# A first batch rearranged: kv products of one head pair by single heads, a sine scaling moved to GpSimd, one weight cast on ScalarE, the last weight slice cast in whole pieces

## Chip, core and metric

Each run used one core of a Trainium2 chip. The metric is the device time of one execution in microseconds (us). The jobs ran on several chips (5, 2, 12 and 3; that of the first job is not on record), so a ratio compares a kernel with the runs of before in its own job. PE is the tensor engine, PEld its weight loads, DVE the vector engine, ACT the scalar engine, POOL GpSimd, SP the engine whose queue issues the loads.

## The reference, cut to what matters

```python
# attention (8 batches, 8 heads, 576 positions, head size 64)
k_p = concat(relu(k) * cos, relu(k) * sin)        # same for q
kv  = einsum('bhsf,bhsd->bhfd', k_p, v);  z = sum(k_p, over s)
out = (q_p @ kv) / (q_p @ z + 1e-6)               # -> x, 4608 tokens x 512
# feed-forward
h = x @ w_in                                      # 512 -> 2048
g = h * sigmoid(beta * h)
return g @ w_out                                  # 2048 -> 512
```

## The kernel before

Tokens go through the feed-forward part in nine chunks of 512. For a chunk PE has 32 slots: 16 column groups of w_in (4 matmuls each), then 16 parts of w_out work. Before chunk 0 there is a head: attention of batch 0, while all weights are still being loaded (as float32, to be cast to bf16 by other engines). The casts of the four w_in slices (column groups 0 to 3, 4 to 7, ...) run on GpSimd and the DVE, just ahead of PE:

```python
def cast_win(i, gj, eng="dve", f0=0, f1=512, jps=slice(0, 2)):   # one of four pieces (g, jj) of slice i, 64 partitions
    ...
def cast_halves(i):
    for f in (0, 256):            # first half of the columns (two column groups), then the second
        for gj in GJ:
            cast_win(i, gj, "dve", f, f + 256)
```

In the head (cut):

```python
v_scale(0, 1, 0, 0, 6, eng="pool")        # sine part of v, head pair 0: 6 of 9 tiles on GpSimd
take("act", 1)
v_scale(0, 1, 0, 6, NQ, eng="act")        # the other 3 on ACT
v_scale(0, 0, 0)                          # cosine part, DVE
k_relu(0, 0, 2, "act", 0, 5);  k_relu(0, 0, 2, "dve", 5, NQ)
take("dve", 0)
kv_mm(0, 0, 6)                            # kv product of pair 0
...
k_relu(0, 2, 3, "act");  k_relu(0, 3, 4, "act", 5, NQ)     # head 2; rest of head 3
...
got = x_rden(2, 0, 0, 7, (0,)); got2 = x_rden(4, 0, 7, 8, (0,))   # denominators, DVE
k_relu(0, 3, 4, "dve", 0, 5)              # head 3, first 5 tiles
warm_pe(2, bank=1)
kv_mm(0, 1, 6)                            # kv product of pair 1: heads 2 and 3 together
```

`warm_pe(n)` puts n idle matmuls on PE, `GJ` lists the four pieces (g, jj) of a slice, `take` copies transposed q out of PSUM, `x_rden` makes the denominators and `x_mul` multiplies by them.

The weights pass through four staging buffers, so a w_out load waits until a w_in slice has been cast:

```python
cast_halves(2); cast_halves(3)
load_w("out", 0); load_w("out", 1)
load_raw(1, "v"); load_raw(1, "k"); load_w("out", 2); load_raw(1, "q"); load_w("out", 3)
```

Of the kernel before, what the change touches and what calls it, by code (L numbers as in the profile page):

```python
# [17 lines left out]
NQ = 9  # L18
# [4 lines left out]
def kernel(  # L23
# [46 lines left out]
    def raw_tile(b, name):  # L70
        if (name, b) not in raws:
            raws[name, b] = raw_pool.tile([P, 4, NQ, D], FP32, name=f"raw_{name}", tag=f"raw_{name}")
        return raws[name, b]
# [14 lines left out]
    def load_w(kind, i, step=4):  # L88
        if (kind, i) not in stages:
            stages[kind, i] = stage.tile([P, 4, 512], FP32, name="w_stage", tag="w_stage")  # L90
        st = stages[kind, i]
        if kind == "out":
            nc.sync.dma_start(out=st, in_=w_out_v[:, 4 * i : 4 * i + 4, :])
            return
        for a in range(0, 4, step):
            nc.sync.dma_start(out=st[:, a : a + step], in_=w_in_v[:, a : a + step, i * 512 : (i + 1) * 512])

    def cast_win(i, gj, eng="dve", f0=0, f1=512, jps=slice(0, 2)):

        g, jj = gj  # L100
        o = win[i].rearrange("q (jp g) f -> q jp g f", g=2)[jj * HP : (jj + 1) * HP, jps, g, f0:f1]
        a = stages["in", i].rearrange("q (jp jj) f -> q jp jj f", jj=2)[g * HP : (g + 1) * HP, jps, jj, f0:f1]
        if eng == "act":
            nc.scalar.copy(o, a)
        elif eng == "pool":
            nc.gpsimd.tensor_copy(o, a)
        else:
            nc.vector.tensor_copy(o, a)  # L108
# [11 lines left out]
    GJ = [(0, 0), (0, 1), (1, 0), (1, 1)]  # L120
# [65 lines left out]
    def relu(dst, src, eng):  # L186
        if eng == "act":
            nc.scalar.activation(dst, src, AF.Relu)  # L188
        else:
            nc.vector.tensor_scalar(dst, src, scalar1=0.0, scalar2=None, op0=ALU.max)  # L190

    def q_relu(b, jp, eng="dve"):
        relu(qb[:, jp].rearrange("q n (j d) -> q j n d", j=2), raw_tile(b, "q")[:, 2 * jp : 2 * jp + 2], eng)

    def k_relu(b, j0=0, j1=4, eng="dve", n0=0, n1=NQ):
        relu(rk.rearrange("q n j d -> q j n d")[:, j0:j1, n0:n1], raw_tile(b, "k")[:, j0:j1, n0:n1], eng)

    def v_scale(b, cs, jp=None, n0=0, n1=NQ, eng="dve"):
        t = (cos9, sin9)[cs]
        rv = raw_tile(b, "v")  # L200
        js = slice(0, 4) if jp is None else slice(2 * jp, 2 * jp + 2)
        if jp is not None and eng != "act":
            if eng == "dve":
                t = ps[:, 0, 16 * cs : 16 * cs + NQ]
            (nc.gpsimd if eng == "pool" else nc.vector).tensor_tensor(
                vb[:, n0:n1, js, cs, 0:D],
                rv.rearrange("q j n d -> q n j d")[:, n0:n1, js],
                t[:, n0:n1].unsqueeze(2).unsqueeze(3).to_broadcast([P, n1 - n0, 2, D]), op=ALU.mult)
            return
        for n in range(n0, n1):  # L210
            o, a = vb[:, n, js, cs, 0:D], rv[:, js, n, :]
            if eng == "act":
                nc.scalar.activation(o, a, AF.Copy, scale=t[:, n : n + 1])  # L213
            else:
                nc.vector.tensor_scalar(o, a, scalar1=t[:, n : n + 1], scalar2=None, op0=ALU.mult)  # L215
# [35 lines left out]
    def kv_out(jp, bank):  # L251
        return ps[:, bank : bank + 2, jp * 2 * E : (jp + 1) * 2 * E]

    def kv_mm(b, jp, bank, jjs=(0, 1)):
        t = kv_out(jp, bank)
        for n in range(NQ):
            for jj in jjs:
                for g in range(2):
                    hs = slice(g * HP, (g + 1) * HP)
                    nc.tensor.matmul(  # L260
                        t[jj * HP : (jj + 1) * HP, g], lhsT=rk[hs, n, 2 * jp + jj, :],
                        rhs=vb[hs, n, 2 * jp + jj].rearrange("q s e -> q (s e)"),
                        start=(n == 0), stop=(n == NQ - 1))

    def kv_take(jps, bank, eng="dve"):
        a0, a1 = jps[0], jps[-1] + 1
        o = kv[:, :, a0:a1].rearrange("q g s c e -> q g (s c e)")
        a = ps[:, bank : bank + 2, a0 * 2 * E : a1 * 2 * E]
        if eng == "act":
            nc.scalar.copy(o, a)  # L270
        else:
            nc.vector.tensor_copy(o, a)  # L272

    def num_mm(n, jp, bank, slot):

        for cs in range(2):
            for jj in range(2):
                rows = slice(jj * HP, (jj + 1) * HP)
                for g in range(2):
                    cols = slice(g * HP, (g + 1) * HP)  # L280
                    nc.tensor.matmul(  # L281
                        ps[cols, bank + jj, slot * E : (slot + 1) * E],
                        lhsT=(qt, qs)[cs][rows, jp, n, cols],
                        rhs=kv[rows, g, jp, cs, :],
                        start=(cs == 0), stop=(cs == 1))

    def x_rden(bank, slot, n0, n1, jps):

        w, m = len(jps), n1 - n0
        nv = ps[:, bank : bank + 2, slot * E : (slot + w * m) * E].rearrange("q j (i s e) -> q j i s e", s=w, e=E)  # L290
        den = small.tile([P, 2, m, w], FP32, name="den", tag=f"den{m}{w}")
        nc.vector.tensor_tensor(  # L292
            den, nv[:, :, :, :, D],
            eps9[:, n0:n1].unsqueeze(1).unsqueeze(3).to_broadcast([P, 2, m, w]), op=ALU.add)
        rden = small.tile([P, 2, m, w], FP32, name="rden", tag=f"rden{m}{w}")
        nc.vector.reciprocal(rden, den)
        return nv, rden, n0, jps

    def x_mul(got, n0, n1):
        nv, rden, first, jps = got  # L300
        a, z, w = n0 - first, n1 - first, len(jps)
        o = xs[:, n0:n1, jps[0] : jps[-1] + 1].rearrange("q n s (j d) -> q j n s d", j=2)
        nc.vector.tensor_tensor(  # L303
            o.rearrange("q j n s d -> q j (n s) d"),
            nv[:, :, a:z, :, 0:D].rearrange("q j n s d -> q j (n s) d"),
            rden[:, :, a:z].rearrange("q j n s -> q j (n s)").unsqueeze(3).to_broadcast([P, 2, (z - a) * w, D]),
            op=ALU.mult)

    def x_mul_act(got, n):
        nv, rden, first, jps = got  # L310
        for s_, jp in enumerate(jps):
            for jj in range(2):
                nc.scalar.activation(xs[:, n, jp, jj * D : (jj + 1) * D], nv[:, jj, n - first, s_, 0:D],
                                     AF.Copy, scale=rden[:, jj, n - first, s_ : s_ + 1])
# [99 lines left out]
    def warm_pe(count, w=512, bank=1):  # L414
        for i in range(count):
            nc.tensor.matmul(ps[:, bank, 0:w], lhsT=zeros[:, 0:P], rhs=zeros[:, 0:w], start=True, stop=True)  # L416
# [24 lines left out]
    warm_pe(7)  # L441
    take("act", 0)
    take("dve", 1)
    v_scale(0, 1, 0, 0, 6, eng="pool")
    take("act", 1)
    v_scale(0, 1, 0, 6, NQ, eng="act")
    v_scale(0, 0, 0)
    k_relu(0, 0, 2, "act", 0, 5)
    k_relu(0, 0, 2, "dve", 5, NQ)
# [4 lines left out]
    kv_take((0,), 6, eng="act")  # L454
    v_scale(0, 1, 1, 5, NQ, eng="act")
    k_relu(0, 2, 3, "act")
    k_relu(0, 3, 4, "act", 5, NQ)
    for i in range(1, 4):
        load_w("in", i)
    warm_pe(1)  # L460
    for n in range(7):
        num_mm(n, 0, 2, n)
    num_mm(7, 0, 4, 0)
    got = x_rden(2, 0, 0, 7, (0,))
    got2 = x_rden(4, 0, 7, 8, (0,))
    k_relu(0, 3, 4, "dve", 0, 5)
    warm_pe(2, bank=1)
    kv_mm(0, 1, 6)
    kv_take((1,), 6, eng="act")
    x_mul(got, 0, 7)  # L470
    x_mul_act(got2, 7)
    warm_pe(1, bank=1)
    for n in range(7):
        num_mm(n, 1, 0, n)
    num_mm(7, 1, 6, 0)
    for gj in GJ:
        cast_win(0, gj, "pool", jps=slice(0, 1))
    for gj in GJ:
        cast_win(0, gj, "pool", 0, 256, slice(1, 2))
    x_turn_pe(0, 0, 8, 2, jps=(0,))  # L480
# [1 line left out]
    x_mul(got, 0, 4)  # L482
    x_mul(got, 4, 7)
    x_mul(x_rden(6, 0, 7, 8, (1,)), 7, 8)
    warm_pe(3, bank=3)
    x_turn_pe(0, 0, 4, 4, ("act",), (1,))
    h_mm(0, 0, (0, 1))
    x_turn_pe(0, 4, 8, 5, ("act",), (1,))
# [5 lines left out]
    def cast_halves(i):  # L494
        for f in (0, 256):
            for gj in GJ:
                cast_win(i, gj, "dve", f, f + 256)
# [3 lines left out]
    def rest():  # L501

        x_mul(x_rden(2, 0, 8, NQ, (0, 1)), 8, NQ)
        cast_halves(2)
        cast_halves(3)
        load_w("out", 0)
        load_w("out", 1)
        load_raw(1, "v")
        load_raw(1, "k")
        load_w("out", 2)  # L510
        load_raw(1, "q")
        load_w("out", 3)
        cast_wout(0)
        cast_wout(1)
        v_scale(1, 0)
        k_relu(1)
        cast_wout(2)
        q_relu(1, 0)
# [111 lines left out]
```

## Time and profile before

| | before |
|---|---|
| time, three runs | 296.96 us (296.57 to 296.97) |
| span of the profiled run | 295.0 us |
| first w_in matmul, first w_out matmul | 18.06, 33.06 us |
| w_out 3 lands; PE's wait for its cast | 45.21 us; 0.33 us |
| second chunk's first matmul | 51.60 us |

All later stages are matmuls without a gap, so the row "second chunk" stands for the end: in the profiles of this study the rest takes 243.2 to 243.9 us.

### The profile page before, as it was taken

Reading aid. Unit: us, or ns where it says so; the run is one execution under the profiler, and the core shown is the slowest. Engines: PE = TensorE matmul, PEld = TensorE weight load, DVE = VectorE, ACT = ScalarE, POOL = GpSimd, SP = SyncE. Lnnn points to the kernel's source line nnn. Section 1 sums busy time; section 2 is a strip of 40 time slices with the busy share of each in tenths; the row PEclk is TensorE's granted clock in tenths of the full one; section 3 lists DMA queues with packets and bytes.
Section 4 is the critical chain, followed back from the end, with each engine's and each line's share of the span. In section 5 each row is a group of like instructions: output and inputs, shape, how many; then the busy total and the mean of one; then the engine's idle time right before and its main releaser. Section 6 shows DMA issues by size and latency. Waiting matters only on the chain.

```text
span 295.0 us, 7173 instructions
## 1 busy us (share of the span) xinstructions
PE 286.8 (97%) x3058; PEld 142.8 (48%) x3058; DVE 116.3 (39%) x296; ACT 140.1 (47%) x223; POOL 73.8 (25%) x88
## 2 busy tenths in 40 slices
PE   8799999999999999999999999999999999999994
PEld 7454455455445544454445544554455444444443
DVE  5989978662920293019500960077005000000000
ACT  5758826563247214731474137512760277137510
POOL 1350003252382026402550256015701210000000
PEclk9999999999999999999999999999999999999999
DMA  7999999597999089916992599139102810130033
GB/s 259 366 393 379 387 389 393 197 288 268 163 259 361 4 125 219 383 62 120 217 379 76 113 231 397 45 67 196 44 2 46 146 37 0 41 84 19 0 73 71
DMA packets 50256, 53.82 MB, mean 182 GB/s; under 512 B 30880, under 2 KB 31152, under 8 KB 50224
## 3 DMA queue, kind: packets, MB, share of 16 engines
q1 hardware_dynamic: 47504, 46.01, 51.6%
q0 software_dynamic: 2688, 7.34, 10.7%
q8 instruction: 24, 0.39, 0.6%
q14 instruction: 8, 0.07, 0.1%
q10 hardware_dynamic: 32, 0.01, 0.0%
HBM read 36.71 MB, written 9.44 MB: 156 GB/s over the span
## 4 chain that ended last, share of the span: by engine, by line
PE 85%; DVE 5%; DMA 5%; ACT 2%; issue 1%; DVEq 0%
PE ps L366 38%; PE ps L391 38%; DMA w_stage<-in_moe_w_out_dram 5%; DVE win L108 4%; PE ps L281 4%; PE ps L260 3%; PE ps L407 1%; PE ps L416 1%; ACT vb L213 1%; DVE qs L218 1%; DVE xs L303 0%; ACT g_t L373 0%; ACT rk L188 0%; PE ps L425 0%; PE ps L230 0%
## 5 line engine op out<-in xcount | busy, mean ns | idle before, releaser
L366 PE MATMUL ps<-xt,win 128*128 128x512 bf16 x576 | 128.1, 379 | 0.8 <-ACT g_t L373 0.5
L391 PE MATMUL ps<-wout,g_t 128*128 128x512 bf16 x560 | 124.5, 379 | 0.2 <-ACT wout L115 0.2
L373 ACT ACTIVATE g_t<-ps,beta 128x512 bf16<-128x512 f32 x144 | 98.4, 687 | 36.6 <-PE ps L366 36.6
L366 PEld LDWEIGHTS <-win 128*128 128x128 bf16 x576 | 55.3, 98 | 67.6 <-DVE win L108 1.4
L391 PEld LDWEIGHTS <-g_t 128*128 128x128 bf16 x560 | 53.9, 98 | 64.0 <-issue 0.4
L386 POOL DMA_DIRECT2D out_dram<-o_sb x56 | 36.5, 656 | 142.2 <-ACT o_sb L397 142.2
L397 ACT COPY o_sb<-ps 128x512 f32<-128x512 f32 x35 | 20.5, 586 | 98.2 <-PE ps L391 98.2
L218 POOL TENSOR_TENSOR qs<-qt,tanr 128x1152 bf16<-128x1152 bf16 x12 | 29.3, 2456 | 10.2 <-DMA qt<-qb 10.2
L272 DVE CAST kv<-ps 128x520 bf16<-128x520 f32 x6 | 4.2, 700 | 67.8 <-PE ps L260 67.8
L410 DVE COPY o_sb<-ps 128x256 f32<-128x256 f32 x1 | 0.4, 425 | 63.0 <-PE ps L407 63.0
L303 DVE TENSOR_TENSOR xs<-ps,rden 128x768 bf16<-128x768 f32 (+5 forms) x26 | 23.1, 890 | 0.8
L292 DVE TENSOR_TENSOR den<-ps,eps 128x12 f32<-128x12 f32 (+4 forms) x26 | 4.2, 161 | 33.5 <-PE ps L281 33.5
L215 DVE TENSOR_SCALAR vb<-raw_v,cos 128x256 bf16<-128x256 f32 x63 | 17.1, 347 | 0.0
L215 DVE TENSOR_SCALAR vb<-raw_v,sin 128x256 bf16<-128x256 f32 x54 | 14.7, 349 | 0.0
L281 PEld LDWEIGHTS <-qt 64*64 64x64 bf16 x576 | 10.6, 106 | 5.0 <-issue 4.3
L281 PE MATMUL ps<-kv,qt 64*64 64x65 bf16 x576 | 11.8, 195 | 0.4 <-ACT kv L270 0.2
L190 DVE TENSOR_SCALAR qb<-raw_q 128x1152 bf16<-128x1152 f32 x16 | 11.4, 752 | 1.3 <-DMA raw_q<-in_q_dram 1.3
L108 DVE CAST win<-w_stage 64x512 bf16<-64x512 f32 (+1 forms) x28 | 11.6, 414 | 0.6
L260 PE MATMUL ps<-vb,rk 64*64 64x130 bf16 x576 | 10.1, 218 | 1.6 <-ACT rk L188 1.6
L281 PE MATMUL ps<-kv,qs 64*64 64x65 bf16 x576 | 11.6, 193 | 0.0
L260 PEld LDWEIGHTS <-rk 64*64 64x64 bf16 x576 | 8.5, 106 | 5.7 <-issue 3.0
L281 PEld LDWEIGHTS <-qs 64*64 64x64 bf16 x576 | 10.4, 105 | 0.0
(56 smaller groups left out, 99.9 us busy)
## 6 DMA issues: line engine op xcount, KB each, us to landing
raw_v<-in_v_dram SPq DMA_DIRECT2D x7, 1152.0 KB, 10.2
raw_k<-in_k_dram SPq DMA_DIRECT2D x7, 1152.0 KB, 12.9
raw_q<-in_q_dram SPq DMA_DIRECT2D x7, 1152.0 KB, 7.4
out_dram<-o_sb POOLq DMA_DIRECT2D x56, 128.0 KB, 4.1
w_stage<-in_moe_w_out_dram SPq DMA_DIRECT2D x4, 1024.0 KB, 9.0
w_stage<-in_moe_w_in_dram SPq DMA_DIRECT2D x3, 1024.0 KB, 12.8
out_dram<-o_sb SPq DMA_DIRECT2D x14, 128.0 KB, 2.3
raw_q<-in_q_dram SPq DMA_DIRECT2D x2, 576.0 KB, 4.4
```

Of the source, the lines that this page charges most:

```text
L108: nc.vector.tensor_copy(o, a)
L190: nc.vector.tensor_scalar(dst, src, scalar1=0.0, scalar2=None, op0=ALU.max)
L215: nc.vector.tensor_scalar(o, a, scalar1=t[:, n : n + 1], scalar2=None, op0=ALU.mult)
L218: eng.tensor_tensor(dst.rearrange("q n (g p) -> q n g p", g=2), src.rearrange("q n (g p) -> q n g p", g=2), tanr[:, n0:n1].unsqueeze(2).to ...
L260: nc.tensor.matmul(t[jj * HP : (jj + 1) * HP, g], lhsT=rk[hs, n, 2 * jp + jj, :], rhs=vb[hs, n, 2 * jp + jj].rearrange("q s e -> q (s e)") ...
L281: nc.tensor.matmul(ps[cols, bank + jj, slot * E : (slot + 1) * E], lhsT=(qt, qs)[cs][rows, jp, n, cols], rhs=kv[rows, g, jp, cs, :], start ...
L303: nc.vector.tensor_tensor(o.rearrange("q j n s d -> q j (n s) d"), nv[:, :, a:z, :, 0:D].rearrange("q j n s d -> q j (n s) d"), rden[:, :, ...
L366: nc.tensor.matmul(ps[:, h_bank(c, jt)], lhsT=win[jt // 4][:, mi, (jt % 4) * P : (jt % 4 + 1) * P], rhs=xt[:, :, jp, g * HP : (g + 1) * HP ...
L373: nc.scalar.activation(g_t, ps[:, h_bank(c, jt)], AF.Silu, scale=beta[:, jt : jt + 1])
L386: eng.dma_start(out=out_v[bb, n][:, m0:m1], in_=o_sb[hf * HP : (hf + 1) * HP, m0:m1])
L391: nc.tensor.matmul(o_ps, lhsT=gs[c, jt][:, tt * P : (tt + 1) * P], rhs=wout[jt // 4][:, jt % 4, :], start=(jt == 0), stop=(jt == JT - 1))
L397: nc.scalar.copy(o_sb, o_ps)
```

## The change

Its intent: free ACT in the head (sine of pair 0 all on GpSimd), start head 2's kv product while head 3 is not ready, let GpSimd end its casts earlier, and save DVE time on the last slice (fewer, larger casts), which also issues the last w_out load earlier. The diff, with context cut:

```diff
-    v_scale(0, 1, 0, 0, 6, eng="pool")
+    v_scale(0, 1, 0, eng="pool")
     take("act", 1)
-    v_scale(0, 1, 0, 6, NQ, eng="act")
...
-    k_relu(0, 3, 4, "act", 5, NQ)
...
     num_mm(7, 0, 4, 0)
+    warm_pe(2, bank=1)
+    kv_mm(0, 1, 6, (0,))
+    k_relu(0, 3, 4, "act", 5, NQ)
     got = x_rden(2, 0, 0, 7, (0,))
     got2 = x_rden(4, 0, 7, 8, (0,))
     k_relu(0, 3, 4, "dve", 0, 5)
-    warm_pe(2, bank=1)
-    kv_mm(0, 1, 6)
+    kv_mm(0, 1, 6, (1,))
+    x_mul_act(got2, 7)
     kv_take((1,), 6, eng="act")
     x_mul(got, 0, 7)
-    x_mul_act(got2, 7)
-    warm_pe(1, bank=1)
...
-        cast_win(0, gj, "pool", jps=slice(0, 1))
+        cast_win(0, gj, "act" if gj == (1, 1) else "pool", jps=slice(0, 1))
...
-    warm_pe(3, bank=3)
+    warm_pe(2, bank=3)
...
         cast_halves(2)
-        cast_halves(3)
+        for gj in GJ:
+            cast_win(3, gj)
```

## The prediction

> **What bounds the kernel now.** I read the page first: busy shares, the chain, the costliest groups. The tensor engine (PE) is busy for 97% of 295.0 us and the chain is matmuls from 56 us to the end, so nothing in the steady part can change: the diff touches only the first batch's set-up and the casts of w_in, all before 32 us. A change there is worth what it moves of the time at which PE gets into that steady run. So I read next the chain in order of time, then the waits and the timeline of the first 56 us, then the landings of the transfers.
>
> The chain that ended last, in order of time, about 12 to 17 us and 31 to 46 us (columns: start us, us, what):
> ```profile
> 11.40 0.73 PE ps L260 x36
> ...
> 12.53 1.18 ACT vb L213 x4
> 13.71 0.57 ACT rk L188
> 14.29 0.04 issue
> 14.33 0.92 PE ps L260 x36
> 15.25 0.02 issue
> 15.27 0.39 ACT kv L270
> 15.66 0.04 issue
> 15.70 0.68 PE ps L281 x48
> ...
> 31.06 0.42 DVE win L108
> 31.48 0.03 issue
> 31.51 13.70 DMA w_stage<-in_moe_w_out_dram
> 45.21 0.02 issue
> 45.24 0.73 ACT wout L115
> 45.97 0.04 issue
> 46.01 1.02 PE ps L391 x4
> ```
> The reader is to see two things. The head is a hand-over between ACT and PE (sin part of v, relu of k, kv product, its copy). And the link at 31.51 us seems to say that the last w_out load starts when the last w_in cast ends, so that earlier casts would bring an earlier load. The next view says otherwise.
>
> Busy time by stretch (PE, PEld, DVE, ACT, POOL, clock, DMA share, GB/s):
> ```profile
> 18.00:24.00 6.00, 5.91 (x46) 2.80 (x45) 5.63 (x18) 4.27 (x8) 1.19 (x3) 1.00 1.05 387
> 24.00:32.00 8.00, 8.00 (x39) 3.25 (x38) 7.61 (x20) 6.29 (x11) 0.00 (x0) 1.00 1.03 374
> 32.00:46.00 14.00, 13.84 (x144) 7.15 (x143) 11.70 (x28) 7.78 (x17) 0.00 (x0) 1.00 1.05 392
> ```
> The DMA engines are full the whole way at 374 to 392 GB/s. In the trace the completions follow one another in the order of issue: w_in slice 3 at 24.44 us, w_out 0 at 27.29, w_out 1 at 29.98, v 33.10, k 36.11, w_out 2 at 38.82, q 41.84, w_out 3 at 45.21. Each comes 2.7 to 3.4 us after the one before, and each was issued long before its predecessor landed (w_out 3 at 31.51, 10 us before q landed). So 13.7 us is queueing: w_out 3 lands at about 45.2 us whenever it is issued. PE is ready for it at 45.68 us (last matmul start 45.465 plus 0.216 of streaming) and starts at 46.01: 0.33 us of waiting. A PE that is earlier at this point gains nothing; one that is later by up to 0.33 us loses nothing.
>
> Groups and waits of the first 56 us:
> ```profile
> L108 DVE CAST win<-w_stage 64x512 bf16<-64x512 f32 x24 | 10.1, 421 | 0.5
> L108 DVE CAST win<-w_stage 64x256 bf16<-64x256 f32 x4 | 1.5, 370 | 0.1
> L205 POOL TENSOR_TENSOR vb<-raw_v,sin 128x768 bf16<-128x768 f32 x1 | 1.5, 1473 | 6.9 <-ACT qt L235 6.9
> ```
> ```profile
> PEld L366 <- DVE win L108: 1.4, 4, 0.4
> ```
> From 26 to 31.5 us PE follows the DVE's casts, but barely: eight casts per slice, half a slice (two column groups) per 1.77 us, against 1.73 us of matmuls (8 by 0.216). The weight loads wait 4 times; the matmul starts in the trace show what reaches PE: 0.17 us at column group 8 (25.83 to 26.22 instead of 0.216) and 0.04 us at groups 10, 12 and 14. PE starts w_out work at 33.06 us.
>
> **What the Trainium skill says.** "SBUF — State Buffer", section "SBUF: two separate sides": DVE and GpSimd share one port pair under an exclusive lock. The trace agrees: a 64x256 cast takes 288 and 292 ns after GpSimd has finished, 472 and 430 ns beside its casts. "VectorE: DVE Perf Modes", the section on the TRN2 errata, measures a fixed part of about 150 cycles, so 512 elements at two per cycle would be (150+256)/0.96 = 423 ns; the row has 421. "TensorEngine Tiling (Array Packing)", "Key Properties": tiles run in parallel. The trace agrees: the kv matmuls start four at a time 3 ns apart, one such step per 56.5 ns, which is the 130 columns. "DMA: Bandwidth & Descriptors", "Queues, rings and completion order", says that descriptors are consumed in ring order on each engine; the landings above agree.
>
> **The change part by part.**
> 1. *Sin of pair 0 all on GpSimd.* ACT loses three 128x128 scalings, 0.99 us by the timeline. GpSimd grows from 768 to 1152 elements: 1473 ns for 768 and 1261 for 640 give 1.66 ns each, so 2.11 us from 9.06, ending near 11.17, or 11.3 if the lock with the DVE's relu (10.43 to 10.85) costs. ACT's relu of k can start when k lands (10.40) instead of 10.63 and ends at 11.15 instead of 11.35. The first kv product then starts at about 11.25, not 11.40: 0.15 us gained, and ACT's next work (bounded by v's landing at 12.14) is earlier by about as much. Head 2's relu ends near 14.13 instead of 14.28.
> 2. *kv of pair 1 by heads.* Before, head 2 was held back by head 3: its first two matmuls went at 14.33, the next at 14.53, after the DVE's relu of head 3 (14.01 + 0.47 = 14.48), and the last at 15.01. Now head 2 can go at 14.18. But one head uses two of four tiles, and a step still streams 130 columns: 9 steps are 0.08 + 8 x 0.0565 = 0.53 us per head, not per pair. Head 3 starts at about 14.66 and its last step at 15.14 us: about 0.13 us later than before. Splitting costs more streaming (0.5 us) than the head start hides (0.3 us). The two ACT scalings of xs move from after the kv copy to before it (0.53 us in ACT's idle time); the filler matmuls removed (0.22 us each) lay in waits. So I take the rest of the head, up to the start of the w_in matmuls, as 0.1 to 0.15 us late.
> 3. *One cast piece on ACT.* GpSimd loses one of four 64x512 pieces at 0.66 us and ends at 18.66 instead of 19.32. ACT takes it in a gap (15.7 to 17.0 us). GpSimd is then done before the DVE's four quarter casts begin: those take 4 x 0.31 = 1.24 us instead of 1.57 (18.55 to 20.12). The DVE's train gains 0.33 us, less the 0.14 of step 2: 0.19. The 0.17 us wait at column group 8 goes.
> 4. *Slice 3 in whole pieces.* Four casts of 64x1024: 421 ns plus 512 elements at the slope of the two rows without contention (421-290 over 256 elements, 0.51 ns) is 0.68, with issue 0.71; four are 2.84 us against eight at 0.443, 3.54. The DVE saves 0.70 us and is free at 30.6 rather than 31.5. But column group 12 needed only the first half, ready at 29.74 us; now it needs all four. The DVE starts the slice at 27.97 - 0.19 = 27.78, the pieces for the first row block are there at 29.2, the others at 30.62. PE is at group 12 at 29.29 + 0.14 = 29.43, does one matmul and waits until 30.66. Then 7 matmuls as before from 31.54 to 33.06 (1.52), plus 8 by 0.216 (1.73): PE starts w_out work at 33.91, not 33.06, 0.8 us late. This is the largest term.
>
> From 33.06 to 45.68 PE has no wait in the trace (only two switches of 0.1 us), so it arrives at w_out 3 at 46.5 us. The slack takes 0.33 of the 0.8. ACT's and the DVE's takes of q lie before their w_out 3 casts and are set by PE, so these casts slip too, to about the same time; the last of the DVE's three may cost another 0.1. Sum: 0.5 to 0.6 us later. The waits at 51.60 (0.39 in matmul starts) and 56.60 (0.66) are for work of ACT that PE itself released, so they move along and absorb nothing.
>
> **The rivals.** *A: hidden by the DMA, no change.* If the casts are fast or the head gains 0.4 us more than I find, PE is late by under 0.33 us, w_out 3 at 45.2 sets the start, and the time stays at 296.9. For it: the full DMA. Against: the 1.2 us between halves and whole pieces at group 12. *B: the earlier issue pays, faster by 0.5 to 0.9 us* (296.2). For it: the chain's link at 31.51. Against: the landing times in order, without a hole, and PE's arrival only 0.33 us before. *C: worse than reckoned*, up to 298.2: if GpSimd's longer sin is blocked by the DVE at 11 us, or the takes of q around 44 us get in the way of the w_out 3 casts.
>
> **Range and chances.** 296.96 plus 0.55 is 297.5 us. Rival A is the low end, 296.6 with the run scatter (296.57 to 296.97); C the high end, 298.2. 2% is 5.9 us, ten times anything here: within 2% at 0.98, faster 0.01, slower 0.01.
>
> **What would show it.** Step 1: the first kv product at 11.2 to 11.35. Step 2: 36 matmuls of pair 1 from about 14.18 and ending no earlier than before; if they end before 15.0, it is wrong. Step 3: quarter casts all near 290 ns. Step 4: four casts of about 690 ns, a gap of some 1.0 to 1.2 us before the second matmul of group 12, w_out work from 33.9. The bound: w_out 3 issued near 30.7 yet landing at 45.2. If it lands before 44.7, rival B is right; if PE still waits for it, rival A.

## The result and the profile after

| | before | after |
|---|---|---|
| time, six runs each | 296.97 us (296.57 to 297.14) | 297.09 us (296.80 to 297.21) |
| profiled run, its span | 295.0 us | 295.4 us |
| first w_in matmul, first w_out matmul | 18.06, 33.06 us | 18.17, 33.84 us |
| w_out 3 issued, landed | 31.51, 45.21 us | 30.56, 44.69 us |
| second chunk's first matmul | 51.60 us | 52.10 us |

The ratio is 1.0004, 95% interval 0.9991 to 1.0017: the same within 2%. A ratio here is the mean time of one kernel's runs over that of the other's runs of the same rounds, so it is not quite the ratio of the medians quoted.

The chain that ended last in the changed kernel, in order of time (start us, us, what):

```profile
9.22 2.12 POOL vb L205
11.35 0.04 issue
11.39 0.73 PE ps L260 x36
...
14.32 1.03 PE ps L260 x36
15.35 0.02 issue
15.38 0.39 ACT kv L270
...
29.84 0.70 DVE win L108
30.54 0.05 issue
30.59 3.41 PE ps L366 x15
34.00 0.86 PE ps L391 x4
```

The link from the w_out load to PE at 45 us is gone. In its place the chain leaves the DVE's casts at 30.54 us, and from there to 50.63 us it is PE's matmuls: column group 12 waits for the last whole piece. Ahead of the first kv product GpSimd's sine has taken ACT's place.

Busy time by stretch in the changed kernel (PE, PEld, DVE, ACT, POOL, clock, DMA share, GB/s):

```profile
24.00:32.00 8.00, 7.18 (x36) 3.19 (x34) 7.73 (x17) 5.75 (x10) 0.00 (x0) 1.00 1.05 385
32.00:46.00 14.00, 13.79 (x144) 7.27 (x144) 10.16 (x24) 7.86 (x17) 0.00 (x0) 1.00 1.05 389
```

PE was busy for 8.00 us of the first stretch, and is now for 7.18: the hole that the prediction named. The DMA engines are as full as before.

Groups and waits of the changed kernel that answer to those of before:

```profile
L108 DVE CAST win<-w_stage 64x512 bf16<-64x512 f32 x16 | 6.7, 421 | 0.3
L108 DVE CAST win<-w_stage 64x1024 bf16<-64x1024 f32 x4 | 2.8, 688 | 0.1
L108 DVE CAST win<-w_stage 64x256 bf16<-64x256 f32 x4 | 1.1, 285 | 0.1
```

```profile
PEld L366 <- DVE win L108: 1.5, 2, 1.3
```

Four casts of 688 ns took the place of eight of 421. The quarter casts fell from 370 to 285 ns. Four short waits of the weight loads for the DVE became two, one of them 1.3 us long; the starts of the matmuls show 0.98 us of it as idle time of PE.

The timeline has one thing that the prediction did not have. The DVE's relu of k for pair 0, first before, then after, then GpSimd's sine after:

```profile
10.43 0.43 DVE L190 TENSOR_SCALAR rk<-raw_k 128x512 bf16<-128x512 f32 x1
```

```profile
10.56 1.06 DVE L190 TENSOR_SCALAR rk<-raw_k 128x512 bf16<-128x512 f32 x1
```

```profile
9.22 2.11 POOL L205 TENSOR_TENSOR vb<-raw_v,sin 128x1152 bf16<-128x1152 f32 x1 [7.06 <-DMA raw_v<-in_v_dram]
```

The same relu takes 1.06 us instead of 0.43. It ends 0.28 us after GpSimd's instruction (9.22 + 2.11 = 11.33). I read this as the DVE being held until GpSimd was through, with the wait standing in the trace as busy time; sin_alone below tests it.

### The profile page after: what moved, and what is told of

Same layout as the page of the kernel before. It is cut to its first block, busy times and chain, and to the rows that moved or that the text cites. A ratio compares the mean times of both kernels' runs of the same rounds, so it can differ in the third digit from the quotient of the medians.

```text
span 295.4 us, 7134 instructions
## 1 busy us (share of the span) xinstructions
PE 283.1 (96%) x3028; PEld 142.8 (48%) x3056; DVE 115.9 (39%) x292; ACT 140.0 (47%) x221; POOL 74.1 (25%) x87
## 4 chain that ended last, share of the span: by engine, by line
PE 87%; DVE 4%; DMA 2%; issue 2%; ACT 2%; POOL 1%; SPq 0%; DVEq 0%; POOLq 0%
PE ps L391 40%; PE ps L366 39%; DVE win L108 4%; PE ps L281 4%; PE ps L260 3%; DMA raw_v<-in_v_dram 2%; PE ps L407 1%; POOL vb L205 1%; DVE xs L303 0%; ACT vb L213 0%; ACT g_t L373 0%; PE ps L230 0%; ACT xt L345 0%; SPq L78 0%; DVE rden L296 0%
## 5 line engine op out<-in xcount | busy, mean ns | idle before, releaser
L391 PE MATMUL ps<-wout,g_t 128*128 128x512 bf16 x535 | 120.3, 379 | 2.3 <-issue 1.4
L190 DVE TENSOR_SCALAR rk<-raw_k 128x2304 bf16<-128x2304 f32 (+2 forms) x9 | 11.0, 1223 | 0.1
L108 DVE CAST win<-w_stage 64x512 bf16<-64x512 f32 (+2 forms) x24 | 10.6, 443 | 0.5
```

Of the source, the lines that this page charges most:

```text
L108: nc.vector.tensor_copy(o, a)
L190: nc.vector.tensor_scalar(dst, src, scalar1=0.0, scalar2=None, op0=ALU.max)
L391: nc.tensor.matmul(o_ps, lhsT=gs[c, jt][:, tt * P : (tt + 1) * P], rhs=wout[jt // 4][:, jt % 4, :], start=(jt == 0), stop=(jt == JT - 1))
```

## The experiments

My theory: PE's arrival at the w_out work sets the end, 33.84 instead of 33.06 us, mostly through the whole pieces; a part is hidden where the last w_out load is late. Rival A: all is hidden behind that load. Rival B: the earlier issue of the load pays. All kernels below gave correct results. The table collects what each profile showed; "w_in stretch" is the time from the first w_in to the first w_out matmul, which leaves out the scatter of the head. Times are in us and from one profiled run each; the ratios are those of the timed runs.

| kernel | first w_in | first w_out | w_in stretch | w_out 3 issued | landed | second chunk | ratio to before (95%) |
|---|---|---|---|---|---|---|---|
| before | 18.06 | 33.06 | 15.00 | 31.51 | 45.21 | 51.60 | 1 |
| after | 18.17 | 33.84 | 15.67 | 30.56 | 44.69 | 52.10 | 1.0004 (0.9991 to 1.0017) |
| after_again | 19.39 | 35.17 | 15.78 | 31.89 | 45.37 | 53.44 | 1.0032 (1.0018 to 1.0045) |
| undo_whole | 18.32 | 32.99 | 14.67 | 31.43 | 44.55 | 51.26 | 1.0001 (0.9986 to 1.0016) |
| whole_alone | 18.01 | 33.98 | 15.97 | 30.70 | 45.08 | 52.25 | 1.0033 (1.0020 to 1.0047) |
| undo_kv_split | 18.18 | 33.92 | 15.74 | 30.64 | 44.80 | 52.18 | 1.0019 (1.0006 to 1.0032) |
| stage5 | 18.16 | 33.19 | 15.03 | 30.04 | 45.51 | 51.90 | 1.0000 (0.9983 to 1.0017) |
| fill1 | 19.37 | 34.48 | 15.11 | 32.71 | 45.82 | 52.75 | 1.0012 (0.9991 to 1.0033) |
| fill4 | 18.00 | 33.88 | 15.88 | 31.47 | 44.76 | 52.15 | 1.0033 (1.0018 to 1.0048) |
| act_piece_alone | 18.40 | 33.08 | 14.68 | 31.52 | 44.73 | 51.35 | 0.9985 (0.9970 to 1.0000) |
| sin_alone | 18.53 | 33.41 | 14.88 | 31.86 | 45.39 | 51.95 | 1.0005 (0.9986 to 1.0025) |
| best1 | 17.89 | 32.57 | 14.68 | 31.01 | 44.31 | 50.88 | 0.9995 (0.9980 to 1.0010) |
| best2 | 18.05 | 32.73 | 14.68 | 31.15 and 32.99 | 43.36 and 45.10 | 51.18 | 0.9989 (0.9973 to 1.0005) |
| best2_again | 17.88 | 32.77 | 14.89 | 31.22 and 33.38 | 43.71 and 45.31 | 51.56 | 0.9990 (0.9977 to 1.0002) |

One rule, taken from the profile of before, fits the others. In before PE needs 12.62 us from the first w_out matmul to the point where it wants w_out 3 (33.06 to 45.68), ACT's cast is usable 0.79 us after the landing (45.21 to 46.00), and from there the second chunk is 5.60 us away. So: second chunk = the later of (first w_out matmul + 12.62) and (landing + 0.79), plus 5.60; where w_out 3 comes in two halves, the landing is that of the first. It gives 52.06 for the changed kernel (measured 52.10), 51.21 for undo_whole (51.26), 52.20 for whole_alone (52.25), 51.90 for stage5 (51.90), 52.10 for fill4 (52.15), 53.39 for after_again (53.44). It is 0.2 to 0.6 short in the three kernels where PE had to wait for q on the way (sin_alone, best2, best2_again).

### The changed kernel timed again (after_again)

No edit.

> The changed kernel as it is, timed in more rounds. My theory (PE starts the w_out work 0.8 us late because column group 12 waits for whole cast pieces; 0.33 us of that is covered by the wait for the last w_out load): 0.2 to 0.6 us slower than before, ratio 1.0005 to 1.002, and in the trace w_out work from 33.8 us with a gap of about 1 us before the second matmul of group 12. Rival A (all hidden behind the load): ratio within 0.0005 of 1, and PE waiting for the w_out 3 cast near 45 us. Rival B (earlier issue pays): under 1.

Measured: 297.67 us (297.09 to 298.47) against 296.87, ratio 1.0032. In the same job, so against the same runs of before, the kernel with the whole pieces alone got 1.0033. The first job had given 1.0004 for the very same kernel. The profiled run of this job (298.47 us) had v's second half landing at 13.46 us instead of 12.03, and with it the whole head 1.2 us later: transfers differ that much from run to run. Over both jobs the 12 runs of the changed kernel have a mean of 297.4 us and the 17 of before 296.8. So the best estimate is that the change costs about 0.5 us. The intervals of the two jobs (-0.3 to 0.5 us and 0.5 to 1.3 us) hardly meet, so the jobs differ by more than the runs within one; a difference between chips is not excluded.

### Halves again in the changed kernel (undo_whole)

```diff
-        for gj in GJ:
-            cast_win(3, gj)
+        cast_halves(3)
```

> The changed kernel with slice 3 again cast in eight half pieces. My theory: the gap at column group 12 goes, PE starts the w_out work at 32.8 to 32.9 us (25.94 plus 32 matmuls of 0.216) instead of 33.83, reaches w_out 3 at about 45.5 and there waits for its cast (load lands 44.7 to 45.2): the end is 0.4 to 1.0 us earlier than the changed kernel and 0 to 0.4 earlier than before. Rival B: without the earlier issue of w_out 3 it lands later, and nothing is gained over the changed kernel. Rival A: same time as both.

The chain that ended last, in order of time:

```profile
28.84 4.32 PE ps L366 x20
33.15 6.04 PE ps L391 x28
```

There is no DVE in the chain between the w_in and the w_out work any more, and the w_in stretch is 14.67 instead of 15.67 us: in the changed kernel the whole pieces cost 1.00 us of PE time. The second chunk starts 0.84 us earlier than in the changed kernel. Timed: 296.64 us, ratio 1.0001 (0.9986 to 1.0016); five of six runs lie between 296.42 and 296.68, one at 297.95. In the same job the changed kernel took 297.67 us, ratio 1.0032 (1.0018 to 1.0045): the two intervals are just apart, so in that job this part accounts for the loss. Rival B is not supported: w_out 3, issued 0.87 us later than in the changed kernel, landed at 44.55, not later. That PE would wait for it was my miss: it landed early enough.

### Whole pieces alone (whole_alone)

```diff
-        cast_halves(3)
+        for gj in GJ:
+            cast_win(3, gj)
```

> The kernel before with slice 3 in whole pieces and nothing else. My theory: w_out work from 33.9 to 34.1 us (the DVE is 0.2 later here than in the changed kernel), PE at w_out 3 at 46.6, after its cast: 0.5 to 0.8 us slower than before, ratio 1.0017 to 1.0027. Rival A: ratio 1.000. Rival B: 0.997 to 0.999, and w_out 3 landing before 44.7.

```profile
29.99 0.70 DVE win L108
30.69 0.05 issue
30.73 3.41 PE ps L366 x15
34.15 6.04 PE ps L391 x28
```

The same chain as in the changed kernel stands here from this edit alone: w_in stretch 15.97 us (0.97 more than before), first w_out matmul at 33.98 us, 297.62 us, ratio 1.0033, more than the 1.0017 to 1.0027 that I expected. Taken out of the change or put into the kernel before, this part is worth 1 us of PE time.

### The same delay without the casts (fill4, fill1)

```diff
+        if slot == 16:
+            warm_pe(4, bank=7)        # fill1: warm_pe(1, bank=7)
```

> The same with four idle matmuls (0.86 us), about what the whole pieces cost at column group 12. My theory: the wait goes and 0.5 to 0.8 us reach the end, ratio 1.0017 to 1.0027, like the kernel with whole pieces alone. Rival A (all hidden behind the load): ratio 1.000.

> The kernel before with one idle 128x512 matmul (0.216 us) ahead of the w_out work. My theory (0.33 us of slack before the w_out 3 cast, if the load lands at 45.2; less if it lands at 44.6): the wait near 45.5 to 46 shrinks by 0.2 and the second chunk starts within 0.1 us of before: ratio 1.000 to 1.0005. Rival (PE sets the time, no slack): 0.22 us later, ratio 1.0007.

Four idle matmuls (0.86 us) gave 297.80 us, ratio 1.0033, and the second chunk at 52.15: a delay of PE of this size reaches the end for the most part, whatever makes it. Rival A falls. In the profiles 0.88 us more of w_in stretch became 0.55 at the second chunk, since before had waited 0.33. The ratio stands for 1.0 us (0.5 to 1.4): the timed runs do not show that anything was hidden, but their lower end leaves room for the 0.33. One idle matmul is inconclusive: 1.0012 with an interval of 0.4%, and its profiled run had the late v (13.45 us), so that its PE was later than the load anyway.

### An earlier issue of the same queue (stage5)

```diff
-    stage = ctx.enter_context(tc.tile_pool(name="stage", bufs=4))
+    stage = ctx.enter_context(tc.tile_pool(name="stage", bufs=5))
```

> The kernel before with five staging buffers for the weights instead of four: each w_out load is issued one cast slice earlier, w_out 3 at about 28 us instead of 31.5; the order of the queue is the same. My theory (the DMA engines are full, 13.7 us is queueing): w_out 3 still lands at 44.5 to 45.4 us, and the time is within 0.3 us of before. Rival B (an earlier issue pays): it lands near 41.7 and PE's wait at 45.7 goes, 0.3 us faster.

The chain that ended last:

```profile
30.04 15.47 DMA w_stage<-in_moe_w_out_dram
45.51 0.02 issue
45.53 0.73 ACT wout L115
46.26 0.04 issue
46.30 1.02 PE ps L391 x4
```

Issued 1.5 us earlier than in before (not 3.5 as I expected: the issue of q in front of it took 5.26 us of the queue), w_out 3 landed 0.3 us later, 15.5 us after its issue, and the time is the same: 296.92 us, ratio 1.0000. Rival B falls. What I had overlooked: the issuing instruction itself took longer the earlier it began (SP's timeline: 30.04 + 2.91 us here, 30.56 + 2.38 in the changed kernel, 31.51 + 1.35 in before), so that it was through at about 32.9 us in all three. Over the kernels with one w_out 3 load the landing lies between 44.31 and 45.82 us without following the issue (31.01, 31.51, 30.04, 30.70 us gave 44.31, 45.21, 45.51, 45.08). It follows what is queued ahead of it: in ten of these twelve profiles it lands 2.66 to 2.72 us after the load of q before it. The other two are before and stage5, with 3.37 and 3.52 us: of the 16 completion steps that the trace has for the load, fifteen were in by 44.51 and 44.68 us, and the last came at 45.21 and 45.51. In these two profiles alone PE waited for it. So the slack of 0.33 us was a straggler in one execution.

### The cast piece on ACT alone (act_piece_alone)

```diff
-        cast_win(0, gj, "pool", jps=slice(0, 1))
+        cast_win(0, gj, "act" if gj == (1, 1) else "pool", jps=slice(0, 1))
```

> The kernel before with the one w_in piece cast on ACT instead of GpSimd, nothing else. My theory: the DVE's four quarter casts take 1.24 us instead of 1.57 because GpSimd has done with the shared port, the waits at column groups 8 to 14 (0.30 us in all) go, w_out work starts at 32.8 instead of 33.06, and PE waits 0.2 to 0.6 us for w_out 3, so that 0 to 0.3 us of it reach the end: ratio 0.999 to 1.000. Rival: the port is not the cause, the quarter casts stay near 370 ns on average.

```profile
L108 DVE CAST win<-w_stage 64x256 bf16<-64x256 f32 x4 | 1.1, 285 | 0.1
```

The quarter casts take 285 ns, PE's gaps at column groups 8 to 14 are gone, and the w_in stretch is 14.68 us, 0.32 shorter. The head of the profiled run was late (18.40), so the first w_out matmul came at 33.08. Timed: 296.30 us against 296.93, ratio 0.9985, interval up to 1.0000. This part is worth 0.3 us in the traces; the timed gain is as large or somewhat larger, at the edge of what four runs show.

### kv of pair 1 in one piece again (undo_kv_split)

```diff
-    kv_mm(0, 1, 6, (0,))
...
-    kv_mm(0, 1, 6, (1,))
+    kv_mm(0, 1, 6)
```

> The changed kernel with the kv product of pair 1 in one piece again (both heads per step). My theory: one pair is 9 steps of 0.0565 us where two heads are 18, but it cannot start before head 3's relu on the DVE (14.58 in the changed kernel): it ends about where the split one ended, 0 to 0.1 us earlier (15.1 instead of 15.17). All later times move by as much, so the end is within 0.1 us of the changed kernel. Rival (the split is what helps): 0.2 us or more later from 15 us on.

PE's timeline of this kernel:

```profile
14.25 0.24 PE L260 MATMUL ps<-vb,rk 64*64 64x130 bf16 x2 [1.06 <-DVE rden L296]
14.66 0.70 PE L260 MATMUL ps<-vb,rk 64*64 64x130 bf16 x34 [0.17 <-DVE rk L190]
```

Joined, head 2 waits for head 3 as before. The last matmul starts at 15.14 us; split, in the changed kernel, at 15.12. In both, and in before, it comes 0.54 us after the end of head 3's relu on the DVE (14.60 to 15.14; 14.58 to 15.12; 14.48 to 15.01). The split neither gains nor costs. The starts of the single matmuls in the changed kernel show why it does not cost: from 14.69 to 14.83 us the starts come 23 and 33 ns apart in turn instead of 56. By count (nine steps each) and by the relu's end (14.58) these are steps of head 3, from 14.64 us on, between head 2's last three; head 3 uses the other two tiles of the array. My expectation had the heads one after the other. Its number was right for another reason (below). The ratio, 1.0019, and that of the changed kernel in the same job, 1.0032, overlap.

### The sine alone (sin_alone)

```diff
-    v_scale(0, 1, 0, 0, 6, eng="pool")
+    v_scale(0, 1, 0, eng="pool")
...
-    v_scale(0, 1, 0, 6, NQ, eng="act")
```

> The kernel before with the sine part of pair 0 all on GpSimd, nothing else. Theory (in the changed kernel the DVE's relu of k took 1057 ns instead of 427 because GpSimd held the shared port until 11.33 us): the relu ends about 0.28 us after GpSimd's 2.11 us instruction whenever that is still running at the relu's start, the following DVE work is 0 to 0.6 us later, and the kv product of pair 1 ends 0.54 us after head 3's relu, 0 to 0.15 later than before; time within 0.2 us of before, ratio 0.9995 to 1.001. Rival (the part gains what ACT is relieved of): first kv product and everything after it 0.15 us earlier, ratio 0.9995 or less.

GpSimd and the DVE in this kernel:

```profile
8.94 2.11 POOL L205 TENSOR_TENSOR vb<-raw_v,sin 128x1152 bf16<-128x1152 f32 x1 [6.77 <-DMA raw_v<-in_v_dram]
```

```profile
10.40 0.93 DVE L190 TENSOR_SCALAR rk<-raw_k 128x512 bf16<-128x512 f32 x1
```

GpSimd ends at 11.05 us and the relu at 11.33, again 0.28 later. In undo_kv_split v landed early, GpSimd ended at 10.45 before the relu began at 10.53, and the relu took 0.42 us. The profiles of undo_whole (0.86 us) and after_again (1.08 us) show the same, each with an end 0.28 us after GpSimd's. So the holding is shown with its cause on both sides. It does not strike every instruction: the DVE's cosine took 1.34 us and GpSimd's sine 1.47 both in before, where the cosine ran wholly beside the sine, and in best1, where they overlapped for 0.57 us. The first kv product moved from 11.40 to 11.10, but pair 1's product waits for later loads (v's second half at 12.60 us here), so nothing of it shows at the end: ratio 1.0005 (0.9986 to 1.0025).

### Versions that the above points to (best1, best2, best2_again)

best1 is before, with the cast piece on ACT and head 3's relu ahead of the denominators on the DVE:

```diff
+    k_relu(0, 3, 4, "dve", 0, 5)
     got = x_rden(2, 0, 0, 7, (0,))
     got2 = x_rden(4, 0, 7, 8, (0,))
-    k_relu(0, 3, 4, "dve", 0, 5)
...
-        cast_win(0, gj, "pool", jps=slice(0, 1))
+        cast_win(0, gj, "act" if gj == (1, 1) else "pool", jps=slice(0, 1))
```

best2 also loads w_out 3 in two halves and gives its four casts to DVE, ACT, DVE, ACT instead of ACT, DVE, DVE, DVE:

```diff
-            nc.sync.dma_start(out=st, in_=w_out_v[:, 4 * i : 4 * i + 4, :])
+            for a in range(0, 4, 2 if i == 3 else 4):
+                z = a + (2 if i == 3 else 4)
+                nc.sync.dma_start(out=st[:, a:z], in_=w_out_v[:, 4 * i + a : 4 * i + z, :])
...
-    cast_wout(3, "addd")
+    cast_wout(3, "dada")
```

> The kernel before with the cast piece on ACT, and head 3's relu on the DVE moved ahead of the two denominators. Theory (the kv product of pair 1 ends 0.54 us after that relu, and the DVE has 0.9 us of idle time behind it): the relu runs at about 13.55 instead of 14.01, the last kv matmul goes at 14.85 instead of 15.01, w_out work starts at 32.65 to 32.9 instead of 33.06, and what w_out 3's landing (44.5 to 45.5) allows reaches the end: 0.3 to 0.7 us faster than before, ratio 0.9977 to 0.999. If the landing bounds it, PE waits about 0.5 us near 45 us and the ratio is 0.9985 to 0.9995.

> The same with the last w_out load in two halves and its first block cast on the DVE (the order DVE, ACT, DVE, ACT). Theory (with an earlier PE, w_out 3 is the bound): the first half lands 1.3 us before the second, PE's wait near 45 us is under 0.2 us, and it is 0.1 to 0.4 us faster than the version without: ratio 0.997 to 0.9985. Rival: ACT's extra casts delay its copies of q, and nothing is gained.

> The version with the cast piece on ACT, the earlier relu and the last w_out load in halves, once more, since six runs left its ratio at 0.9989 with an interval that holds 1. Theory (PE reaches w_out 3 about 0.4 us earlier than before and its first half is there): w_out work from 32.6 to 32.9 us, no wait near 45 us, ratio 0.9975 to 0.9995. Rival (no real gain): ratio 0.9995 to 1.0005.

best1: the relu at 13.35 us, the last kv matmul at 14.84, the first w_out matmul at 32.57, the second chunk at 50.88, 0.72 us earlier than in the profile of before. Timed: 296.49 against 296.51 us, ratio 0.9995: the profile's gain is not seen in the timed runs, and the 0.3 to 0.7 us that I expected did not come. best2: 296.29 and, in another job, 296.47 us; ratios 0.9989 and 0.9990. Two jobs agree on 0.1%, about 0.3 us, and each interval still holds 1, so it is probable and not shown that this version beats the kernel before. Against the changed kernel it was not timed in the same rounds; the changed kernel's own ratios to before were 1.0004 and 1.0032. In best2_again PE waited for an earlier load of the queue, that of q, which landed at 42.38 us:

```profile
43.22 0.68 PE L232 MATMUL ps<-ident,qb 128*128 128x128 bf16 x9 [0.40 <-DVE qb L192]
```

PE stood still for 0.57 us there, and for 0.23 in best2 (starts of the matmuls). In these profiles an earlier PE meets the full DMA queue at another load; that this bounds every change of the head is not shown.

## Why the prediction was right or wrong

The prediction was 297.5 us, 296.6 to 298.2; measured were 297.09 us in the first job and 297.67 in the second. The range held, and the two jobs lie on either side of the center. But the range is wide enough to hold the time of before too, and 297.09 by itself is nearer to rival A's 296.9; it is the traces and the second job that speak for the mechanism.

- **Bound and DMA.** Right: the chain's link at 31.51 us was queueing and not a start that casts could bring forward (stage5). Too narrow: "lands at about 45.2 us whenever it is issued". It landed between 44.3 and 45.8 from run to run. My own sign for rival B, a landing before 44.7, came true by a hair (44.69) with rival B false; the sign was badly chosen, since it was inside this scatter.
- **Step 1, the sine.** Half wrong. GpSimd's duration was right (2.11 us), but the first kv product came at 11.39 and not 11.25 us: v had landed 0.16 us later. Nothing of what ACT was relieved of reached head 2, whose kv product began at 14.32 as in before (14.33) and not at 14.18. The lock fell on the other side than I reckoned: not GpSimd but the DVE's relu was held, 0.63 us, and then the cosine of pair 1 began at 12.27 instead of 12.16 and head 3's relu at 14.11 instead of 14.01.
- **Step 2, kv by heads.** Right number (last matmul 15.14 forecast, 15.12 measured), wrong reason, so the agreement is luck. The 0.1 us came from that late relu; the heads' streams overlap and the split is neutral.
- **Step 3, the cast piece.** Right: GpSimd was done at 18.60 us, before the quarter casts began at 18.66, and these took 285 ns; 0.32 us less in the w_in stretch where it stands alone.
- **Step 4, whole pieces.** Right: 688 ns each (0.68 forecast), a gap of 0.98 us before the second matmul of group 12, first w_out matmul at 33.84 (33.91 forecast). In the w_in stretch they cost 1.00 us, in either direction of the test. (The prediction's 423 ns for a 64x512 cast is an estimate from the fixed part that it cites; the rows have 421.)
- **The sum.** The term that was mis-sized is the slack of 0.33 us before w_out 3. It belonged to one execution in which the load landed late (two of twelve profiles have such a wait). In the profile pair it holds: 0.78 us at the first w_out matmul, 0.50 at the second chunk. Where the load lands near 44.6, the rule above has none; the 0.86 us of filler cost 1.0 (0.5 to 1.4), which does not decide it. Why the first job showed only 0.1 us between the kernels, and the second 0.9, stays open: the trace of the second has late transfers, but the other runs have no trace, and the jobs may differ in the chip.

## What to carry to other kernels

A cast just ahead of its user should be cut in the order in which it is used: fewer and larger pieces saved the DVE 0.7 us and cost PE 1.0. A long arrow from a DMA in the chain of waits says when the load was asked for, not what bounds it; look at whether the loads before it land back to back. And before work goes to GpSimd, see what the DVE has to do meanwhile: here its work held up a relu by 0.6 us.

## What the Trainium skill lacked or had wrong

- "SBUF — State Buffer", section "Who interferes with whom", says that of GpSimd and a DVE instruction in a mode with two ports the second "fully blocks", and these runs agree. It lacks how that looks in a profile: the waiting is inside the DVE's busy time. A relu of 0.42 us is recorded as 0.86 to 1.08 us in four profiles, ends 0.28 us after GpSimd's instruction in all of them, and has at most 0.03 us of idle time before it.
- "TensorEngine Tiling (Array Packing)", section "Key Properties", has tiles that run in parallel. No page has that matmuls on other tiles can then start ahead of some that precede them in the kernel's program order: by the count of steps, head 3's matmuls started from 14.64 us among head 2's, which went on to 14.80, with starts 23 and 33 ns apart in turn instead of 56.
